# A spatial gating product by seven half-size products per pair of token tiles in place of eight, on one core of Trainium2

## The chip, the cores and the metric

The kernel runs on one core of one Trainium2 chip. A core has five engines with instruction queues of their own: TensorE (PE in the profile; its weight loads are shown apart as PEld), VectorE (DVE), ScalarE (ACT), GpSimd (POOL) and SyncE (SP), which here only issues DMA transfers. Matrix products are written to PSUM, eight banks of 128 partitions by 512 float32 numbers; everything else lies in SBUF. Engines run their own instructions in order and wait for one another by semaphores. The metric is the device time of one launch, in microseconds.

## What is computed

The input x has 2048 tokens of 512 numbers. Two branches are mixed by a gate of each token, `g * a + (1 - g) * b`.

```
# branch a: linear attention, 32 heads of 16
pq, pk = q @ w_phi, k @ w_phi                    # per head
phi = concat([softmax(p), softmax(-p)])          # 32 features
kv, z = sum_s phi_k * v,  sum_s phi_k
a = (phi_q @ kv / (phi_q . z + 1e-6)) @ wo
# branch b: spatial gating, F/2 = 688
z = gelu(x @ w_in); z1, z2 = z[:, :688], layernorm(z[:, 688:])
gate = w_sp @ z2 + b_sp                          # w_sp: 2048 x 2048, over tokens
b = (z1 * gate) @ w_out
```

The change concerns above all `w_sp @ z2`, a product of 2048 x 2048 by 2048 x 688.

## The kernel before

Tokens are handled in 16 tiles of 128. All data is 16-bit (bf16), sums are float32 in PSUM.

The first stage (lines 212 to 334) makes z2 and z1 for four chunks of four tiles. For each z2 tile ScalarE applies gelu, VectorE copies the gate's logit (L204) and takes the mean and variance (L206, L207). `z2_norm` (L262) then has GpSimd compute the reciprocal deviation (L267, `rstd`) and VectorE normalise the four tiles in place (L269). Meanwhile SyncE's queue loads w_sp transposed into `wspT`, 16 slabs of 128 input tokens by 2048 output tokens, in four transfers of 512 output tokens (L154).

The second stage is the loop over 16 key tiles (L580). For each: TensorE multiplies out the next key tile (`k_tile`, L373), ScalarE makes exp(p) and exp(-p) (L356), VectorE sums them per head (L360) and inverts (L376). `even_out` (L366) scales the second half of the features on GpSimd (L369) by the ratio of the two sums (VectorE, L368); the rest of the normalisation is put on v, which VectorE reads out of PSUM (L397). `kv_acc` (L405) adds the tile to the state two tiles later. In each round `gg_next` adds one half-row of the spatial product (`gg_half`, L448): 16 matmuls of 344 columns over all 16 slabs, read out of PSUM by VectorE as (product + bias) * z1 into `ucat` (L456). Six query tiles are also made here (`Q_AT`).

The third stage (L602) makes in each round one query tile, one half-row of the spatial product, one attention tile (L461) and one output tile (`ba_step`, L550). `kvz_evac` (L413) hands the state over between the stages. u, o and eq are transposed by DMA on SyncE's queue. The last 48 of the 688 rows of w_out are handled for four output tiles together (`ba_rem`, L515), next to an attention tile that is split into halves of 64 rows (`attn_tile_64`, L471).

The order of the work on TensorE and ScalarE is the order in which it is written (`manual_schedule`, L576); that on VectorE, GpSimd and SyncE is set by a planner when the program is built. PSUM: in stages two and three six banks rotate under the names mm0 to mm5, two hold the state or an attention tile.

## Time and profile before

| what | value |
| --- | --- |
| three timed executions | 206.29, 206.67, 206.68 us (median 206.67) |
| the profiled execution's span, first to last instruction | 204.3 us; what lies around it up to the median is 2.4 us |
| TensorE busy | 200.5 us in 1557 matmuls |
| VectorE busy | 130.4 us, of it 58.4 from 43.5 to 117 us |
| GpSimd busy | 45.6 us, of it 25.8 from 43.5 to 117 us |
| spatial product's matmuls (L451) | 512, 2.33 us for 16 in the chain of waits |
| granted TensorE clock | 1.000 |

The page names engines and lines; a group `out<-in` gives what is written and read, with partitions x elements and type, the count, the busy time in us, the mean of one in ns, and the engine's idle time just before. A timeline's line begins with start and length in us. Where several instructions are merged (x4), the length is that of them all.

### The profile page before, as it was taken

The numbers are of one execution on the slowest core, as the hardware profiler recorded it, in microseconds if no ns is written. First come the engines' busy times: TensorE is split into PE (matmuls) and PEld (weight loads), VectorE is DVE, ScalarE is ACT, GpSimd is POOL, SyncE is SP. The second block draws the span as 40 slices with busy tenths as digits, with TensorE's granted clock in tenths as the row PEclk, the third lists the DMA queues.
The fourth block names the chain that finished last, engine by engine and source line by source line (L and its number), as shares of the span: only waits on it lengthen the run. The fifth ranks groups of instructions, "written<-read, shape, count | busy, mean of one in ns | idle before, by whom it ended". The sixth has DMA issues, their size and how long they took to land.

```text
span 204.3 us, 3996 instructions
## 1 busy us (share of the span) xinstructions
PE 200.5 (98%) x1557; PEld 119.7 (59%) x1557; DVE 130.4 (64%) x283; ACT 74.6 (37%) x122; POOL 45.6 (22%) x76
## 2 busy tenths in 40 slices
PE   8999999999999999999999999999999999999994
PEld 4666666655665555656565666555555555665642
DVE  4558484838977597979797789555566645633332
ACT  3556677795222333342424042222351136002303
POOL 3020202022523325424242442222204220200000
PEclk9999999999999999999999999999999999999999
DMA  6999399999999027941322229763667458552943
GB/s 200 232 176 153 65 207 232 219 290 231 259 240 232 3 39 158 311 94 21 70 52 41 51 39 115 141 130 59 110 160 80 90 114 183 64 96 51 139 81 104
DMA packets 89947, 27.22 MB, mean 133 GB/s; under 512 B 84200, under 2 KB 89928, under 8 KB 89928
## 3 DMA queue, kind: packets, MB, share of 16 engines
q1 hardware_dynamic: 87616, 24.81, 63.5%
q10 hardware_dynamic: 2312, 2.16, 3.8%
q8 instruction: 12, 0.20, 0.4%
q14 instruction: 7, 0.06, 0.1%
HBM read 4.15 MB, written 2.10 MB: 31 GB/s over the span
## 4 chain that ended last, share of the span: by engine, by line
PE 94%; DMA 4%; SPq 1%; DVE 0%; issue 0%
PE mm L451 37%; PE zp L188 16%; PE mm L352 14%; PE mm L512 9%; PE mm L506 7%; PE mm L392 7%; DMA w_z<-in_B_w_in_dram 2%; PE kvacc L408 2%; PE at L464 2%; DMA xs<-in_A_x_dram 1%; PE mm L517 1%; SPq L131 1%; PE zp L304 0%; SPq L136 0%; PE at L475 0%; PE pq L304 0%
## 5 line engine op out<-in xcount | busy, mean ns | idle before, releaser
L451 PE MATMUL mm<-z2all,wspT 128*128 128x344 bf16 x512 | 79.9, 309 | 0.0
L451 PEld LDWEIGHTS <-wspT 128*128 128x128 bf16 x512 | 49.0, 98 | 25.3
L188 PE MATMUL zp<-w_z,xT 128*128 128x344 bf16 (+1 forms) x254 | 38.1, 309 | 0.1
L356 ACT ACTIVATE eq<-mm 128x512 bf16<-128x512 f32 x32 | 17.4, 595 | 51.4 <-PE mm L352 25.7
L360 DVE TENSOR_REDUCE zs<-eq 128x64 f32<-128x1024 bf16 x16 | 19.5, 1220 | 20.1 <-ACT eq L356 20.1
L188 PEld LDWEIGHTS <-xT 128*128 128x128 bf16 x254 | 24.5, 98 | 12.1 <-issue 0.3
L356 ACT ACTIVATE ek<-mm 128x512 bf16<-128x512 f32 x32 | 17.3, 601 | 27.1 <-PE mm L352 27.1
L456 DVE SCALAR_TENSOR_TENSOR ucat<-mm,bT,z1all 128x344 bf16<-128x344 f32 x32 | 17.4, 544 | 15.1 <-PE mm L451 15.1
L369 POOL TENSOR_TENSOR eq<-eq,ratio 128x512 bf16<-128x512 bf16 x16 | 16.9, 1055 | 44.6 <-DVE ratio L368 36.7
L528 ACT ACTIVATE ob<-mm,g_inv 128x512 bf16<-128x512 f32 (+1 forms) x15 | 10.1, 680 | 33.1 <-PE mm L517 28.5
L360 DVE TENSOR_REDUCE zs<-ek 128x64 f32<-128x1024 bf16 x16 | 19.2, 1208 | 2.8 <-ACT ek L356 2.8
L512 PE MATMUL mm<-wspT,uT 128*128 128x512 bf16 (+2 forms) x85 | 20.1, 367 | 0.0
L352 PEld LDWEIGHTS <-xT 128*128 128x128 bf16 x128 | 12.2, 98 | 12.0
L369 POOL TENSOR_TENSOR ek<-ek,ratio 128x512 bf16<-128x512 bf16 x16 | 16.9, 1055 | 2.2 <-DVE ratio L368 1.7
L506 PE MATMUL mm<-wspT,oT 128*128 128x512 bf16 (+2 forms) x68 | 16.6, 366 | 0.0
L352 PE MATMUL mm<-wq_p,xT 128*128 128x512 bf16 x64 | 16.4, 379 | 0.0
L392 PE MATMUL mm<-wv_sb,xT 128*128 128x512 bf16 x64 | 16.4, 379 | 0.0
L352 PE MATMUL mm<-wk_p,xT 128*128 128x512 bf16 x64 | 16.3, 379 | 0.0
L206 DVE BATCH_NORM_STATS2 bn<-z2all 128x6 f32<-128x344 bf16 x32 | 14.9, 502 | 0.0
L203 ACT ACTIVATE z2all<-zp 128x688 bf16<-128x688 f32 x16 | 11.8, 743 | 7.1 <-PE zp L188 7.0
L257 ACT ACTIVATE z1all<-zp 128x688 bf16<-128x688 f32 x16 | 11.9, 743 | 5.3 <-PE zp L188 4.9
L512 PEld LDWEIGHTS <-uT 128*128 128x128 bf16 x85 | 8.1, 98 | 9.4 <-issue 0.2
(77 smaller groups left out, 142.0 us busy)
## 6 DMA issues: line engine op xcount, KB each, us to landing
out_dram<-ob ACTq DMA_DIRECT2D x12, 128.0 KB, 2.6
wspT<-in_B_w_out_dram SPq DMA_DIRECT2D x2, 640.0 KB, 5.2
w_z<-in_B_w_in_dram SPq DMA_DIRECT2D x2, 344.0 KB, 4.1
wv_sb<-in_A_wqkv_dram SPq DMA_DIRECT2D x1, 512.0 KB
wspT<-in_A_wo_dram SPq DMA_DIRECT2D x2, 256.0 KB, 4.1
out_dram<-ob SPq DMA_DIRECT2D x3, 128.0 KB, 1.8
w_z<-in_B_w_in_dram ACTq DMA_DIRECT2D x2, 172.0 KB, 3.3
w_z<-in_B_w_in_dram SPq DMA_DIRECT2D x2, 172.0 KB, 3.1
```

Source lines behind the costliest of these rows:

```text
L188: nc.tensor.matmul(zp[:, j, 0:n], lhsT=xT[:, dt, tt * P:(tt + 1) * P], rhs=wt[:, dt, j * HF:j * HF + n], start=(dt == 0), stop=(dt == NDT ...
L206: nc.vector.bn_stats(out=bn6[:, tt, j, :], in_=z2v[:, j, :])
L257: nc.scalar.activation(out=z1all[:, tt, :].rearrange("p (j n) -> p j n", j=2), in_=zp[:, :, 0:HF], func=AF.Gelu_apprx_tanh,)
L352: nc.tensor.matmul(ps[:, :], lhsT=xT[:, dt, tt * P:(tt + 1) * P], rhs=w[:, dt, :], start=(dt == 0), stop=(dt == NDT - 1))
L356: nc.scalar.activation(out=e[:, :, a, :], in_=ps[:, :].rearrange("p (h f) -> p h f", f=DH), func=AF.Exp, scale=1.0 - 2.0 * a)
L360: nc.vector.tensor_reduce(out=z[:].rearrange("p h a -> p (h a)"), in_=e[:].rearrange("p h a f -> p (h a) f"), axis=AX.X, op=ALU.add,)
L369: nc.gpsimd.tensor_tensor(out=e[:, :, 1, :], in0=e[:, :, 1, :], in1=ratio[:, :, None].to_broadcast([P, H, DH]), op=ALU.mult)
L392: nc.tensor.matmul(v_ps[:, :], lhsT=xT[:, dt, tt * P:(tt + 1) * P], rhs=wv_sb[:, dt, :], start=(dt == 0), stop=(dt == NDT - 1))
L451: nc.tensor.matmul(gp[:, 0:HF], lhsT=wspT[:, st, tt * P:(tt + 1) * P], rhs=z2all[:, st, j * HF:(j + 1) * HF], start=(st == 0), stop=(st == ...
L456: nc.vector.scalar_tensor_tensor(out=ucat[tt % NU][:, c0 + j * HF:c0 + (j + 1) * HF], in0=gp[:, 0:HF], scalar=bT[:, tt:tt + 1], in1=z1all[ ...
L506: nc.tensor.matmul(acc, lhsT=oTs[tt][:, g, :], rhs=wo_t[:, g, c0:c1], start=start and g == 0, stop=stop and g == NG - 1)
L512: nc.tensor.matmul(acc, lhsT=uTs[tt][:, i + ft, :], rhs=w_main[i][:, ft, c0:c1], start=start and ft == 0, stop=False)
```

## The change

The 16 x 16 blocks of w_sp and the two column halves of z2 are grouped in pairs: two output tiles (rows 1 and 2), even and odd input slabs, two halves of 344 columns. With A11, A12 (row 1, even and odd slabs), A21, A22 (row 2) and B11, B12 (even slabs, column halves), B21, B22 (odd slabs), a pair of output tiles is eight products of eight matmuls over slabs. The change uses Strassen's scheme in Winograd's form with seven: A11 B11, A12 B21, S1 T1, S2 T2, S3 T3, S4 B22, A22 T4, where S1 = A21 + A22, S2 = S1 - A11, S3 = A11 - A21, S4 = A12 - S2, and T1 = B12 - B11, T2 = B22 - T1, T3 = B22 - B12, T4 = B21 - T2. A product's chain is called below by its first factor: chain s2 is S2 T2, chain s4 is S4 B22. In the notation of the code x, y and z are the banks gx, gy and gz.

- `z2_norm` makes the T for its two pairs of slabs with four tensor_tensor operations of 688 elements on VectorE, one of them in place over B12.
- `s_sums` makes the S of a pair of output tiles with four tensor_tensor operations of 1024 elements; S1 takes the place of A21. Those of pair 0 run on VectorE behind the last of `z2_norm`, those of pair 1 on GpSimd behind the last `rstd`, the others on VectorE at the end of the pair two before.
- `products` issues the seven chains of a pair one at a time, in three PSUM banks (gx, gy, gz) that are added into twice or three times, with read-outs between. ScalarE copies the first product; VectorE has six read-outs of 344 columns; GpSimd multiplies 688 and 344 elements by z1. The result u lies in `z1all`, widened to 768 columns, and is transposed into the columns of `wspT` that the pair has used up. Two chains per round replace one half-row, but every fourth round of the key stage has one.
- Keys are normalised by GpSimd over all 1024 features (`k_tile`) with no ratio; v is copied out of PSUM by ScalarE.
- Key, value and query products rotate over three PSUM banks in place of six, four query tiles instead of six are made in the key stage, and the shared remainder and the split attention tile go: each output tile has six full matmuls for u.

```diff
+        zq = z2all[:, ts[0]:ts[-1] + 1, :].rearrange("p (k s) (j n) -> p k s j n", s=2, j=2)
+        tq = tz[:, ts[0] // 2:ts[-1] // 2 + 1]
+        b11, b12, b21, b22 = (zq[:, :, s, j, :] for s in range(2) for j in range(2))
+        for o, a, b in ((tq[:, :, 1, :], b22, b12), (b12, b12, b11),
+                        (tq[:, :, 0, :], b22, b12), (tq[:, :, 2, :], b21, tq[:, :, 0, :])):
+            on_dve = nc.vector.tensor_tensor(out=o, in0=a, in1=b, op=ALU.subtract)
+        return on_dve, on_pool
...
+    def s_sums(p, eng):
+        st = gg.tile([P, 3, 8, P], BF16, name="ssum")
+        a11, a12, a21, a22 = (a_block(p, i, j) for i in range(2) for j in range(2))
+        s2, s3, s4 = (st[:, n] for n in range(3))
+        for o, a, b, op in ((s3, a11, a21, ALU.subtract), (a21, a21, a22, ALU.add),
+                            (s2, a21, a11, ALU.subtract), (s4, a12, s2, ALU.subtract)):
+            eng.tensor_tensor(out=o, in0=a, in1=b, op=op)
+        s_tiles[p] = st
...
+        for p, eng in enumerate((nc.vector, nc.gpsimd)):
+            with tc.issue_after(last[p].ins):
+                s_sums(p, eng)
...
-        return bank_tile(next_turn("mm", 6))
+        return bank_tile(next_turn("mm", 3))
...
-        ek, z = expo(kvp, "ek", 5, tt, wk_p, mm_tile())
-        rk = kvp.tile([P, H, 2], FP32, name="rk", bufs=3)
-        nc.vector.reciprocal(out=rk[:], in_=z[:])
-        even_out(ek, z, rk[:, :, 1])
-        return ek, rk
+        ek, z = expo(kvp, "ek", 4, tt, wk_p, mm_tile())
+        nc.vector.reciprocal(out=z[:], in_=z[:])
+        nc.gpsimd.tensor_tensor(
+            out=ek[:], in0=ek[:], in1=z[:, :, :, None].to_broadcast([P, H, 2, DH]), op=ALU.mult)
+        return ek
...
+        vr = vrs[tt % 3]
+        nc.scalar.copy(out=vr[:, :, 0:64], in_=v_ps[:, :].rearrange("p (u n) -> p u n", n=64))
...
+    def chain(tag, a, b, first, last=True):
+        if first:
+            gt[tag] = bank_tile(tag)[:, 0:HF]
+        for k in range(8):
+            nc.tensor.matmul(gt[tag], lhsT=a[:, k, :], rhs=b[:, k, :], start=first and k == 0,
+                             stop=k == 7, skip_group_check=True)
+        return gt[tag]
+
+    def products(p):
...
+        x = chain("gx", a11, b11, True)
+        nc.scalar.copy(out=p1[:], in_=x)
+        yield
+        y = chain("gy", s2, tt2, True)
+        nc.vector.scalar_tensor_tensor(
+            out=u2[:], in0=y, scalar=bT[:, t1:t1 + 1], in1=p1[:], op0=ALU.add, op1=ALU.add)
+        yield
+        chain("gx", a12, b21, False)
+        nc.vector.scalar_tensor_tensor(
+            out=z1all[:, t1, 0:HF], in0=x, scalar=bT[:, t1:t1 + 1], in1=z1all[:, t1, 0:HF],
+            op0=ALU.add, op1=ALU.mult)
+        yield
+        chain("gy", s3, tt3, False)
+        nc.vector.scalar_tensor_tensor(
+            out=u3[:], in0=y, scalar=bT[:, t2:t2 + 1], in1=p1[:], op0=ALU.add, op1=ALU.add)
+        yield
+        z = chain("gz", s1, tt1, True)
+        nc.vector.tensor_tensor(out=g2[:, 1, :], in0=z, in1=u3[:], op=ALU.add)
+        yield
+        chain("gy", a22, tt4, False)
+        nc.vector.scalar_tensor_tensor(
+            out=g2[:, 0, :], in0=y, scalar=bT[:, t2:t2 + 1], in1=p1[:], op0=ALU.add, op1=ALU.add)
+        nc.gpsimd.tensor_tensor(
+            out=z1all[:, t2, 0:FH], in0=z1all[:, t2, 0:FH], in1=g2[:].rearrange("p j n -> p (j n)"),
+            op=ALU.mult)
+        u_T(t2)
+        yield
+        chain("gz", s4, b22, False)
+        nc.vector.tensor_tensor(out=g1[:], in0=z, in1=u2[:], op=ALU.add)
+        nc.gpsimd.tensor_tensor(
+            out=z1all[:, t1, HF:FH], in0=z1all[:, t1, HF:FH], in1=g1[:], op=ALU.mult)
+        u_T(t1)
+        if p + 2 < NP2:
+            s_sums(p + 2, nc.vector)
+        yield
...
-                ks[tt + 1] = k_tile(tt + 1)
-            ek, rk = ks.pop(tt)
-            pend.append((tt, ek, v_tile(tt, rk)))
+                ks[tt + 1] = k_tile(tt + 1)
+            gg_next(1)
+            pend.append((tt, ks.pop(tt), v_tile(tt)))
             if len(pend) == 3:
                 kv_acc(*pend.pop(0))
-            gg_next(mm_tile())
+            gg_next(0 if tt % 4 == 3 else 1)
...
+            gg_next(1)
+            attn_tile(i + 1)
+            gg_next(1)
```

## The prediction

> **What bounds the kernel now.** I read the page's busy shares and slices first. The third line names the slices of the stage that computes keys and values (44 to 117 us).

> ```profile
> PE 200.5 (98%) x1557; PEld 119.7 (59%) x1557; DVE 130.4 (64%) x283; ACT 74.6 (37%) x122; POOL 45.6 (22%) x76
> ...
> DVE  4558484838977597979797789555566645633332
> ```

> TensorE (PE) is busy from end to end, so work taken off it is gained only if nothing makes it wait. VectorE (DVE) averages 64%, but 7 to 9 tenths in the key and value stage. Next the groups by line and shape, for prices:

> ```profile
> L451 PE MATMUL mm<-z2all,wspT 128*128 128x344 bf16 x512 | 79.9, 309 | 0.0
> ...
> L360 DVE TENSOR_REDUCE zs<-ek 128x64 f32<-128x1024 bf16 x16 | 19.2, 1208 | 2.8 <-ACT ek L356 2.8
> L456 DVE SCALAR_TENSOR_TENSOR ucat<-mm,bT,z1all 128x344 bf16<-128x344 f32 x32 | 17.4, 544 | 15.1 <-PE mm L451 15.1
> ...
> L369 POOL TENSOR_TENSOR ek<-ek,ratio 128x512 bf16<-128x512 bf16 x16 | 16.9, 1055 | 2.2 <-DVE ratio L368 1.7
> ...
> L397 DVE TENSOR_TENSOR vr<-mm,rk 128x512 bf16<-128x512 f32 x16 | 10.9, 684 | 3.2 <-PE mm L392 3.2
> ```

> Zero idle before L451: the 512 matmuls never waited. Then the timeline where GpSimd (POOL) and VectorE touch:

> ```profile
> 113.22 1.06 POOL L369 TENSOR_TENSOR eq<-eq,ratio 128x512 bf16<-128x512 bf16 x1
> 113.46 0.87 DVE L368 TENSOR_TENSOR ratio<-zs,rk 128x32 f32<-128x32 f32 x1
> ```

> The ratio, whose two inputs both lie in SBUF, takes 0.87 us and ends at 114.33, just behind the GpSimd operation (114.28). In the tile's answer its median is 193 ns:

> ```profile
> L368 DVE TENSOR_TENSOR ratio<-zs,rk x16: 139/193/874, 50.0 to 113.5; 128x32 f32<-128x32 f32 x16
> ```

> All six key ratios that start while GpSimd's tensor_tensor runs took 848 to 874 ns; L397 and L456, with one input in PSUM, keep their times there. So VectorE's two-SBUF-input operations and GpSimd's take turns, whole instructions at a time. Last, the timeline where the spatial product begins:

> ```profile
> 41.45 1.04 POOL L267 TENSOR_TENSOR rstd<-veps,mhalf 128x4 f32<-128x4 f32 x1
> 42.52 1.56 DVE L269 TENSOR_SCALAR z2all<-z2all,mv,rstd 128x688 bf16<-128x688 bf16 x4 [1.47 <-POOL rstd L267]
> ...
> 43.49 1.89 PE L352 MATMUL mm<-wk_p,xT 128*128 128x512 bf16 x8
> ...
> 46.08 2.50 PE L451 MATMUL mm<-z2all,wspT 128*128 128x344 bf16 x16
> ```

> **TensorE's work.** A run of 16 L451 matmuls advances 2.33 us in the chain of waits, 0.146 us each; 512 become 448: 64 x 0.146 = -9.3 us. The remainder matmuls shared by four tiles go: in the timeline L517 starts at 145.23 and the next q product at 145.96, 0.73 us for four remainders and a split attention tile (0.82 with the delay in front); instead come four full matmuls (0.216 each: five L512 in 1.08) and eight L464 (0.26), 1.12. Three such groups at +0.3 and +0.2 in the last: +1.1. Net -8.2 us: with no wait anywhere, 206.67 - 8.2 = 198.5.

> **Prices of the new operations.** *GpSimd:* L396 (32 elements, 0.212) and L369 (512, 1.055) give 1.76 ns an element: a sum of s_sums or a whole key tile (1024) 1.95 us, the products with z1 1.36 (688) and 0.76 (344). *VectorE, 16-bit tensor_tensor with both inputs in SBUF:* no row. L269's four take 1.56 (0.37 a step for 688), so 0.55 us for 1024; L397 slopes to 1.22 for 1024. I take 0.61 and 0.44 (688), near L269, which like the new ones is 16-bit and SBUF to SBUF; 1.22 and 0.8 stay as the other end. [...] *PSUM evacuations:* as L456, 0.5 a step.

> **What is nearly free.** ScalarE takes the v copy (0.58, as L311) and p1: per key tile 2 x 0.6 + 0.6 + 0.1 = 1.9 of 4.0 us. VectorE loses L397 and the key ratios (0.68 + 0.44 per tile) and gains per pair six evacuations for four and four sums: about even in time, but the sums are lock-takers. The differences of z2_norm (1.8 us per chunk) in the first three chunks fall into the 1.5 us VectorE idles before the next glog copy: 0 to 0.3 us. On SP the same 16 u transposes now go into dead columns of wspT, each waiting for a GpSimd product (0.8 to 1.4 us); behind them in SP's order stand eqT and oT transposes, which are used two iterations later (some 11 us at 5.6 of TensorE's work each), so this costs nothing until GpSimd is that late; then attention and output tiles wait. The weight loads go one key tile later and lose a 640 KB and a 48 KB piece; they are first read after the last key tile, 30 us on. GpSimd loses the four small kvz copies.

> **The start of the product, +8.1 us.** TensorE comes to the second chain (s2 by T2) at 43.5 + 1.7 (two key tiles) + 1.2 (first chain) + 0.9 (v) = 47.2. VectorE must by then have done four normalisations (1.5), four differences (1.8) and three sums (1.8), from 42.5: 47.6 alone, 0.4 late. But GpSimd issues the four sums of pair 1 at 42.9, right behind rstd and three small memsets (its wspT part has landed: L451 reads it at 46.1). Each operation in both lists waits on its predecessor's semaphore, which opens a gap in which the other engine gets its turn. With turns, GpSimd's four (7.8) lie among VectorE's first eight, and s2 is ready at 42.5 + 5.1 + 7.8 = 55.4: TensorE loses 8.1, some 2.7 at the first chain (last normalisation), the rest at the second. Bounds: 0.4 if GpSimd waits instead; 11.4 at the slow price (four times 0.36 and three times 0.6 more).

> **Each later pair, +2.2 us.** Between chain s4 of a pair and chain s3 of the next, TensorE has three v, two k, three kv, two x and one y runs: 8.6 us. In the built order VectorE does there g1, two reciprocals, four sums, one key reduce and u2: 0.5 + 1.0 + 2.4 + 1.2 + 0.5 = 5.6. GpSimd then has a key tile (1.95), both z1 products (2.1) and soon another key ready; turns put 3 to 4 us between the sums. 9 to 9.5 against 8.6: With each pair's own list (pairs 2 and 3 carry q reduces, but also q products of 0.9 on TensorE) it comes to 0.3, 0.6, 0.8, 0.5 late at pairs 0 to 3. Bounds: 0 without turns, 9 at the slow price (2.4 more in each pair, less in pair 0).

> **The state's hand-over, +3.2 us.** The sums of pair 5 stand ahead of kvz_evac on VectorE. From pair 3's last chain to attention tile 0 TensorE has v, q and three kv (2.5) and two chains (2.3): 4.8. VectorE: g1 0.5, sums 2.4, kvz 0.7, and a q reduce (1.2) ahead of kvz's second half: 4.8; GpSimd's eq and z1 turns add 3.2. Bounds: 0.4 without turns, 5.4 with sums 0.6 longer.

> **Small, +1.2 us:** pair 3's z is read behind two reduces and two reciprocals, 0.7 late; two attention tiles 0.25 each behind sums.

> Sum: -8.2 + 8.1 + 2.2 + 3.2 + 1.2 = +6.5. The durations are of an execution with a span of 204.3; 2.4 us lie around it up to the median 206.67, and I leave them. Forecast **213.2 us**, 3% slower.

> [...]

> **Rivals.**
> 1. *VectorE keeps the port while it has operations in a row, and GpSimd waits.* For it: L269's four run 0.37 us apart without a gap. Against: the new sums wait on each other, and the two directions are seen only from VectorE's side. The start then costs 0.4 plus 2.0 for the first key tile (GpSimd is done with pair 1's sums only at 56), the hand-over 1.1 to 1.4 (one turn each way), the pairs and the small waits 2 to 3.7: -8.2 + 5.4 to 7.5 gives 203.9 to 206. This one ends on the other side; it decides where the start costs under 1.6 us (8.2 less 6.6 elsewhere), that is if not even one GpSimd sum gets in front of s2.
> 2. *All waits are covered,* GpSimd's turns being short: only the 2 us of waits that the order makes without turns: 200.5.
> 3. *The 16-bit tensor_tensor runs at L397's rate.* Start 11.4, the pairs 9, hand-over 5.4, later pairs 3: about 227.

> **How the numbers follow.** The forecast's case holds 0.60 (211 to 218: GpSimd prices 10% either way move it by 2, and a slower restart lies above), rival 1 0.24, rival 2 0.08, rival 3 0.08. The likeliest case alone spans 210 to 218. The range goes down into rival 2 and leaves rival 3 out: 200.5 to 219. Changes under 0.2% (0.4 us) are what a measurement here cannot tell from none. Faster: rivals 1 (nearly all) and 2, with the forecast's lower tail: 0.29; same 0.03; slower 0.68.

> **What would show it.** TensorE idle before the first chain and the s2 chain at 47 to 56 us, released by VectorE; rstd followed by four GpSimd sums that alternate with L278 and L294, some of these lasting 2 us; L436 late. If the VectorE sums keep 0.6 us and GpSimd's stretch, rival 1 holds. The forecast is wrong if GpSimd's sums are much shorter than 1.95, or if VectorE's are over 1.

## The result, and the profile after

The changed kernel takes **216.7 us** (median of four executions, 214.75 to 219.21) against 206.6 in the same session: ratio 1.047, 95% interval 1.042 to 1.052. It is 4.7% slower. The longest of the four, 219.21, counts as a slow execution and is not in the ratio. The forecast was 213.2, its range 200.5 to 219. The profiled execution has a span of 215.1 us, 10.8 more than before.

The busy shares, the granted clock by slices and the chain that ended last, from the page of the changed kernel:

```profile
PE 197.5 (92%) x1469; PEld 115.8 (54%) x1469; DVE 156.9 (73%) x304; ACT 88.4 (41%) x147; POOL 86.7 (40%) x76
...
PEclk9999999997579999999999996999999999999999
...
PE 69%; DVE 21%; DMA 4%; ACT 2%; POOL 2%; issue 1%; SPq 0%; DVEq 0%; POOLq 0%; ACTq 0%
```

TensorE has 88 matmuls fewer but is busy only 3 us less, in a span that is longer: a fifth of the last chain is now VectorE's, and the second line has two dips. In the kernel before it has none:

```profile
PEclk9999999999999999999999999999999999999999
```

What TensorE waits for (line, releaser, us in total, times, longest):

```profile
PE gy L467 <- DVE ssum L294: 7.1, 1, 7.1
PE at L533 <- DVE kvz L441: 2.9, 1, 2.9
PE gx L467 <- DVE z2all L268: 1.0, 1, 1.0
...
PE gy L467 <- DVE u L489: 0.5, 2, 0.3
PE pq L326 <- DVE bT L315: 0.5, 1, 0.5
PE mm L551 <- ACT ob L568: 0.5, 1, 0.5
PE gz L467 <- DVE g L502: 0.4, 1, 0.4
```

One wait of 7.1 us stands out, the second chain of pair 0. The timeline there (start, length, engine, line):

```profile
43.67 7.03 DVE L268 TENSOR_SCALAR z2all<-z2all,mv,rstd 128x688 bf16<-128x688 bf16 x4 [1.47 <-POOL rstd L266]
...
43.78 2.32 POOL L294 TENSOR_TENSOR ssum<-wspT 128x1024 bf16<-128x1024 bf16 x1
...
46.19 2.12 POOL L294 TENSOR_TENSOR wspT<-wspT 128x1024 bf16<-128x1024 bf16 x1
...
48.55 0.31 PE L467 MATMUL gx<-z2all,wspT 128*128 128x344 bf16 x1 [1.00 <-DVE z2all L268]
...
50.58 2.12 POOL L294 TENSOR_TENSOR ssum<-wspT,ssum 128x1024 bf16<-128x1024 bf16 x1
50.73 2.34 DVE L278 TENSOR_TENSOR tz<-z2all 128x688 bf16<-128x688 bf16 x1
53.10 0.52 DVE L278 TENSOR_TENSOR z2all<-z2all 128x688 bf16<-128x688 bf16 x1
...
54.64 0.69 DVE L294 TENSOR_TENSOR ssum<-wspT 128x1024 bf16<-128x1024 bf16 x1
...
56.83 2.48 PE L467 MATMUL gy<-tz,ssum 128*128 128x344 bf16 x8 [7.11 <-DVE ssum L294]
```

Four normalisations that took 1.56 us before take 7.03, and the first difference 2.34 where the others take 0.52. GpSimd's four sums follow one another at 2.2 to 2.4 us; one VectorE instruction gets through between two of them. When GpSimd is done (52.70), VectorE ends the first difference (53.07) and needs 3.7 us more for the other three and three sums; the chain starts at 56.83. It then takes 2.48 us for eight matmuls, 1.33 elsewhere: the clock is halved from 51.43 to 61.67.

The hand-over of the state, with pair 5's sums ahead of `kvz_evac` (L436, L441):

```profile
123.64 1.95 POOL L507 TENSOR_TENSOR z1all<-z1all,g 128x688 bf16<-128x688 bf16 x1
...
124.26 1.87 DVE L294 TENSOR_TENSOR wspT<-wspT 128x1024 bf16<-128x1024 bf16 x1
...
125.55 1.29 POOL L514 TENSOR_TENSOR z1all<-z1all,g 128x344 bf16<-128x344 bf16 x1
...
128.63 1.21 DVE L388 TENSOR_REDUCE zs<-eq 128x64 f32<-128x1024 bf16 x1
...
129.83 0.18 DVE L441 SCALAR_TENSOR_TENSOR kvz<-kvacc,mask 128x32 bf16<-128x32 f32 x1
...
130.16 0.61 PE L533 MATMUL at<-kvz,eqT 128*128 128x68 bf16 x8 [2.92 <-DVE kvz L441]
...
130.58 1.90 PE L380 MATMUL mm<-wq_p,xT 128*128 128x512 bf16 x4
```

VectorE's sums are stretched to 1.87 us and GpSimd's products to 1.95 and 1.29 (1.50 and 0.84 where nothing stands against them). The turns go both ways. Again the matmuls behind the wait run at half the clock: 1.90 us for the four of a query product, 1.03 elsewhere.

### The profile page after: what moved, and what is told of

It is laid out like the page before. It is cut to its first block, busy times and chain, and to the rows that moved or that the text cites. A ratio compares the mean times of both kernels' runs of the same rounds, so it can differ in the third digit from the quotient of the medians.

```text
span 215.1 us, 3862 instructions
## 1 busy us (share of the span) xinstructions
PE 197.5 (92%) x1469; PEld 115.8 (54%) x1469; DVE 156.9 (73%) x304; ACT 88.4 (41%) x147; POOL 86.7 (40%) x76
## 4 chain that ended last, share of the span: by engine, by line
PE 69%; DVE 21%; DMA 4%; ACT 2%; POOL 2%; issue 1%; SPq 0%; DVEq 0%; POOLq 0%; ACTq 0%
PE gy L467 13%; PE mm L380 12%; PE mm L556 9%; PE gz L467 8%; PE gx L467 7%; PE mm L551 6%; PE zp L187 6%; DVE z2all L268 5%; PE mm L421 4%; DVE bn L205 4%; DVE tz L278 3%; DVE ssum L294 3%; DMA w_z<-in_B_w_in_dram 2%; PE at L533 2%; DVE zs L388 2%; POOL rstd L266 1%
## 5 line engine op out<-in xcount | busy, mean ns | idle before, releaser
L397 POOL TENSOR_TENSOR ek<-ek,zs 128x1024 bf16<-128x1024 bf16 x16 | 32.4, 2025 | 25.9 <-DVE zs L396 16.1
L407 POOL TENSOR_TENSOR eq<-eq,ratio 128x512 bf16<-128x512 bf16 x16 | 17.4, 1088 | 46.6 <-DVE ratio L406 29.6
L467 PEld LDWEIGHTS <-wspT 128*128 128x128 bf16 x256 | 24.6, 99 | 15.0 <-issue 1.1
L467 PE MATMUL gy<-tz,ssum 128*128 128x344 bf16 x128 | 22.4, 320 | 7.7 <-DVE ssum L294 7.1
L568 ACT ACTIVATE ob<-mm,g_inv 128x512 bf16<-128x512 f32 (+1 forms) x16 | 10.9, 680 | 44.1 <-PE mm L556 40.8
L467 PEld LDWEIGHTS <-ssum 128*128 128x128 bf16 x192 | 18.4, 99 | 19.0 <-DVE ssum L294 7.6
L388 DVE TENSOR_REDUCE zs<-ek 128x64 f32<-128x1024 bf16 x16 | 19.3, 1208 | 8.1 <-ACT ek L384 6.8
L384 ACT ACTIVATE eq<-mm 128x512 bf16<-128x512 f32 x32 | 17.4, 595 | 18.9 <-PE mm L380 16.0
L467 PE MATMUL gx<-z2all,wspT 128*128 128x344 bf16 x128 | 22.4, 318 | 1.0 <-DVE z2all L268 1.0
L556 PE MATMUL mm<-wspT 128*128 128x512 bf16 (+1 forms) x96 | 22.8, 376 | 0.0
L380 PEld LDWEIGHTS <-xT 128*128 128x128 bf16 x128 | 12.6, 101 | 12.9 <-issue 1.1
L380 PE MATMUL mm<-wq_p,xT 128*128 128x512 bf16 x64 | 17.3, 394 | 0.0
L551 PE MATMUL mm<-wspT,oT 128*128 128x512 bf16 (+1 forms) x64 | 16.2, 376 | 0.7 <-ACT ob L568 0.5
L268 DVE TENSOR_SCALAR z2all<-z2all,mv,rstd 128x688 bf16<-128x688 bf16 x16 | 11.7, 796 | 5.9 <-POOL rstd L266 5.9
L424 ACT CAST vr<-mm 128x512 bf16<-128x512 f32 x16 | 9.4, 586 | 15.9 <-PE mm L421 15.9
L556 PEld LDWEIGHTS <-wspT 128*128 128x128 bf16 x102 | 9.8, 98 | 11.2
```

What stands on the lines that cost most here:

```text
L268: nc.vector.tensor_scalar(out=z2all[:, tt, :], in0=z2all[:, tt, :], scalar1=mv[:, tt, 0:1], scalar2=rstd[:, tt:tt + 1], op0=ALU.subtract, ...
L380: nc.tensor.matmul(ps[:, :], lhsT=xT[:, dt, tt * P:(tt + 1) * P], rhs=w[:, dt, :], start=(dt == 0), stop=(dt == NDT - 1))
L384: nc.scalar.activation(out=e[:, :, a, :], in_=ps[:, :].rearrange("p (h f) -> p h f", f=DH), func=AF.Exp, scale=1.0 - 2.0 * a)
L388: nc.vector.tensor_reduce(out=z[:].rearrange("p h a -> p (h a)"), in_=e[:].rearrange("p h a f -> p (h a) f"), axis=AX.X, op=ALU.add,)
L397: nc.gpsimd.tensor_tensor(out=ek[:], in0=ek[:], in1=z[:, :, :, None].to_broadcast([P, H, 2, DH]), op=ALU.mult)
L407: nc.gpsimd.tensor_tensor(out=eq[:, :, 1, :], in0=eq[:, :, 1, :], in1=ratio[:, :, None].to_broadcast([P, H, DH]), op=ALU.mult)
```

## The experiments

The question was where the saved 8.2 us of TensorE went. *Theory:* into two placements, pair 1's sums on GpSimd just when VectorE has the start to do, and pair 5's sums ahead of the hand-over, together with the lowered clock behind the two pauses. *Rival:* into the sums themselves, which cost their turns wherever they are put.

### Pair 1's sums on VectorE

```diff
-        for p, eng in enumerate((nc.vector, nc.gpsimd)):
-            with tc.issue_after(last[p].ins):
-                s_sums(p, eng)
+        with tc.issue_after(last[0].ins):
+            s_sums(0, nc.vector)
...
+            if tt == 2:      # one sum of pair 1 behind each of four read-outs of pair 0
+                s_sums_behind(1, [(m, 0) for m in ("z1", "u3", "g21", "g20")])
```

> Edit: the four sums of pair 1 are taken off GpSimd and put on VectorE, one each behind four read-outs of pair 0. If turns at the SBUF port make the start late (the theory): VectorE runs its four normalisations, four differences and three sums without a gap, 4 x 0.37 + 4 x 0.54 + 3 x 0.72 = 5.9 us from 43.7, so the second chain starts near 49.7 instead of 56.8, some 1.1 us late instead of 8.4, the clock stays full there (another 2.4), and the four sums cost up to 1 us at later read-outs: 206.5 to 208. If VectorE's own new work were late (rival A): the second chain stays near 56.8 and the time at 216 or above, since VectorE gets four operations more.

Measured: 210.33 us (median of four), ratio 1.022 (1.017 to 1.026). The profiled execution, 213.1, is the longest of the four. Its timeline at the start:

```profile
44.22 1.56 DVE L268 TENSOR_SCALAR z2all<-z2all,mv,rstd 128x688 bf16<-128x688 bf16 x4 [1.48 <-POOL rstd L266]
...
50.10 1.34 PE L477 MATMUL gy<-tz,ssum 128*128 128x344 bf16 x8 [0.99 <-DVE ssum L305]
```

and at the places to which the sums went:

```profile
57.92 2.16 POOL L407 TENSOR_TENSOR ek<-ek,zs 128x1024 bf16<-128x1024 bf16 x1 [0.48 <-DVE zs L406]
...
58.70 1.93 DVE L296 TENSOR_TENSOR wspT<-wspT 128x1024 bf16<-128x1024 bf16 x1
...
62.23 1.33 PE L477 MATMUL gz<-z2all,ssum 128*128 128x344 bf16 x8 [1.21 <-DVE g L512]
...
74.13 1.55 PE L477 MATMUL gy<-tz,ssum 128*128 128x344 bf16 x8 [2.00 <-DVE u L499]
```

The start came out as expected: normalisations unbroken, the second chain 0.99 us late in place of 7.11, no halved clock there. But the time is 2 to 4 us over the expectation. The moved sums wait behind GpSimd's key divisions (1.93 us for one), and a new wait of 1.21 follows. Another, of 2.00, comes behind the sums of pair 2 (one of them takes 2.30); in the changed kernel these cost no more than 0.3, and that the moved sums brought VectorE and GpSimd into this order is likely, not shown. The hand-over's wait of 2.9 us is as before. The profiled execution has two stretches of halved clock, behind these last two waits; by their mean granted clock (0.991 and 0.992 in place of 0.984) the three others, at 210.2 to 210.4, had one. The start is settled as the largest cost. That the sums could be had elsewhere for nothing is refuted.

### Only writes on GpSimd

```diff
+            if eng is nc.gpsimd:
+                for _ in range(2):
+                    eng.memset(o, 0.0)
+            else:
+                eng.tensor_tensor(out=o, in0=a, in1=b, op=op)
```

> Edit: each of GpSimd's four sums of pair 1 is replaced by two memsets of its output, so the sums of pair 1 are left out and GpSimd is busy about as long (eight of some 1 us) but reads nothing in SBUF. Theory (the port that both read through): VectorE's normalisations step by 0.37 us, the second chain starts near 49.7, time some 207. Rival C (a busy GpSimd delays something else, such as the first keys): the second chain is early but TensorE waits 5 us or more at the first state products, time above 212. If memsets take turns too, the normalisations stretch to about 1 us each and the second chain starts near 55.

Measured: 210.0 us (one execution), 3 us above what the theory had and below the rival's 212. Its timeline:

```profile
43.28 2.03 POOL L296 MEMSET wspT<- 128x1024 bf16 x2
43.36 4.43 DVE L268 TENSOR_SCALAR z2all<-z2all,mv,rstd 128x688 bf16<-128x688 bf16 x4 [1.47 <-POOL rstd L266]
...
45.56 5.91 POOL L296 MEMSET ssum<- 128x1024 bf16 x6
...
47.82 0.52 DVE L278 TENSOR_TENSOR tz<-z2all 128x688 bf16<-128x688 bf16 x1
...
49.90 0.69 DVE L298 TENSOR_TENSOR ssum<-wspT 128x1024 bf16<-128x1024 bf16 x1
...
52.10 2.48 PE L471 MATMUL gy<-tz,ssum 128*128 128x344 bf16 x8 [3.85 <-DVE ssum L298]
```

The two kinds of VectorE operation part here. The normalisation (one input in SBUF and one number per partition) takes turns even with an operation that only writes: 4.43 us for four, 1.56 with nothing against them. The differences and sums (two inputs in SBUF) run beside the memsets at 0.52 and 0.69 as if alone. So the expectation failed for the normalisations, which stretched as its last sentence had it, and held for the rest: the second chain starts at 52.10, between its 49.7 and 55. In the changed kernel, where GpSimd's sums read SBUF, both kinds waited (7.03 us for the four normalisations, 2.34 for the first difference). So it is neither GpSimd's instruction count nor its queue, but what each operation does at the memory. Why writes alone hold up the one kind and not the other is not shown, and the port of the expectation stands in no view.

### The same sums on GpSimd, later

```diff
+        scrap1 = pers.tile([P, 1], BF16, name="scrap1")
+        turn1 = nc.gpsimd.tensor_copy(out=scrap1[:, :], in_=s_tiles[0][:, 2, 7, P - 1:P])
+        with tc.issue_after(turn1.ins):
+            s_sums(1, nc.gpsimd)
```

> The changed kernel with one edit: pair 1's four sums stay on GpSimd, all four, but behind a one-column copy that reads the last sum of pair 0, so that they begin when VectorE's work for the start is over. Theory (it is their falling together with VectorE's start work that costs, not that GpSimd makes them): VectorE's normalisations unbroken, the second chain of pair 0 about 1.2 us late, no lowered clock there. The price appears on GpSimd: four sums of 2.12 us end near 59.5 us, the first key tile is divided 2 us later, near 61.5, and the first kv accumulation (due near 59.5 by the trace with pair 1's sums placed on both engines) waits 2 to 3 us; hand-over as in the changed kernel, 3.1 us, and the lowered clock there. Together 7.3 + 2.4 - 1.2 won at the start (the clock in it) and 2 to 3 given back on the changed kernel's 216.7 (span 215.1): 208.5 to 211.5. Rival (GpSimd's sums cost the same wherever they stand, since they delay the keys by as much): 213 or more.

Measured: 214.18 us (four executions), ratio 1.036 (1.033 to 1.039), where the rival had put it. What TensorE waits for:

```profile
PE kvacc L433 <- POOL ek L400: 3.1, 1, 3.1
PE at L536 <- DVE kvz L444: 2.9, 1, 2.9
PE gy L470 <- DVE u L501: 2.0, 1, 2.0
PE gy L470 <- DVE ssum L294: 1.0, 1, 1.0
```

The start is cured here too (1.0), so the falling together did cost what it seemed to. But four sums are 8.7 us of GpSimd, and the keys stand behind them: the first accumulation waits 3.1. The second step was missed in the expectation: VectorE, held in its queue at a key reduction for 7.3 us until the first division was over, reads pair 0 out late (2.0), and a stretch of halved clock (60.99 to 67.81) begins in the first wait and holds the second. Just behind the start GpSimd had no room for all four.

### The hand-over alone

```diff
-        if p + 2 < NP2:
+        if p + 2 < NP2 and p != 3:
...
-        kvz_evac()
+        with tc.issue_after(kvz_evac().ins):
+            s_sums(5, nc.vector)
```

> Edit: the four sums of pair 5 are issued behind the state's hand-over on VectorE instead of ahead of it. If those sums and GpSimd's turns between them delay the hand-over (the theory): TensorE's 3.1 us wait at attention tile 0 falls to under 0.6 and the second drop of the clock (1.25 us) goes with it: 212.3 to 213. If the state itself is late (rival B: GpSimd's normalising of the last key tiles, or a q reduce): the wait stays at 2 us or more and the time above 215.5.

Measured: 214.49 us, ratio 1.038 (1.035 to 1.041): 0.9% off the changed kernel's ratio of 1.047, but 1.5 us above the theory's range. The wait of 2.9 us at the first attention tile is gone and so is the second stretch of halved clock, but the sums now hold up the attention's read-out:

```profile
131.29 0.41 PE L533 MATMUL at<-kvz,eqT 128*128 128x68 bf16 x8 [1.58 <-DVE o L538]
```

Half of the wait moved on by one tile. With the sums spread, as in the version with both placements moved below, 0.2 of it is left.

### The clock alone

36 matmuls whose result nobody reads fill the pause before the second chain; nothing gets earlier.

```diff
+        if p == 0:
+            idle = bank_tile("gy")[:, 0:HF]
+            for k in range(36):
+                nc.tensor.matmul(idle, lhsT=a11[:, k % 8, :], rhs=b11[:, k % 8, :], start=True, stop=True,
+                                 skip_group_check=True)
```

> Edit: 36 matmuls of 344 columns whose result is overwritten are put in front of the second chain, 5.3 us of work inside TensorE's 7.3 us pause. They do not move the second chain (56.8). If the pause costs more than itself because the granted clock halves from 51.4 to 61.7 us (theory): the clock stays at 1.00 there, the second chain and what follows run at 0.146 and 0.216 us a matmul: 2.4 us less, 214.3. If the halved clock costs nothing that ends late (rival D): 216.7.

Measured: 214.86 us, ratio 1.040 (1.038 to 1.043), 1.8 us less by medians and 2.2 by the spans (212.9). The second chain started 0.2 us earlier (56.66), as the first stage had ended that much earlier, and ran in 1.34 us in place of 2.48. From its start to the wait at the hand-over TensorE needs 68.2 us, in the changed kernel 70.4. The halved clock at the start costs about 2 us by itself.

### Keys and values alone, in the kernel before

```diff
-        even_out(ek, z, rk[:, :, 1])
...
+        nc.gpsimd.tensor_tensor(
+            out=ek[:], in0=ek[:], in1=z[:, :, :, None].to_broadcast([P, H, 2, DH]), op=ALU.mult)
...
+        nc.scalar.copy(out=vr[:, :, 0:64], in_=v_ps[:, :].rearrange("p (u n) -> p u n", n=64))
```

> The kernel before with one part of the change alone: keys divided by both sums on GpSimd (1024 elements in place of 512), v copied from PSUM by ScalarE with its ones columns set once, no ratio for the keys. Eight half products of 16 matmuls as before. Theory (GpSimd and ScalarE have room in the stage of keys, and TensorE waits for neither): GpSimd's key operations 2.0 us each, no new wait of TensorE over 0.3 us, 206.2 to 206.9 us, the same as before (206.5) within 0.2%. Rival (the keys arrive too late for the accumulation, or the longer GpSimd operations hold up VectorE's ratio for the queries): kv accumulation waits for the last keys at the hand-over by 1 us or more, 207.5 us or more.

Measured: 206.31 us in twelve executions, ratio 0.9995 (0.9983 to 1.0008): no difference. GpSimd's division takes 1.93 us each, VectorE is busy 115.8 us in place of 130.4, and TensorE waits for nothing. This part of the change costs nothing by itself, and takes 15 us off VectorE.

### Both placements moved

Pair 1's first two sums stay on GpSimd behind the gate of the run above, the other two go to VectorE, one behind each of two read-outs; `kvz_evac` gets ahead, and pair 5's sums are issued two behind each of the first two attention read-outs (`s_part(p, n, eng)` issues the n-th sum of pair p).

```diff
+        with tc.issue_after(turn1.ins):
+            s_part(1, 0, nc.gpsimd)
+            s_part(1, 1, nc.gpsimd)
...
+                with tc.issue_after(read[('u2', 0)].ins):
+                    s_part(1, 2, nc.vector)
+                with tc.issue_after(read[('g21', 0)].ins):
+                    s_part(1, 3, nc.vector)
...
+        with tc.high_priority():
+            kvz_evac()
...
+                with tc.issue_after(read[('o', 0)].ins):
+                    s_part(5, 0, nc.vector)
+                    s_part(5, 1, nc.vector)
```

> Three moves together, nothing else altered: of pair 1's four sums the first two stay on GpSimd but are queued behind a one-column copy that reads the last sum of pair 0, so that they begin only when VectorE's work for the start is over; the other two go to VectorE, one behind the u2 and one behind the g2 of pair 0; kvz_evac goes ahead of everything that VectorE has at the hand-over, and pair 5's four sums go behind the first two attention tiles. Theory (the change lost its gain to the two placements, the start and the hand-over, and not to the sums as such): the four normalisations before pair 0's sums in one unbroken 1.6 us, the second chain about 1.2 us late, no pause long enough to lower the granted clock, the waits before later pairs 1 to 2.5 us together, the hand-over under 0.8 us. With the full TensorE floor of 198.5 us and the 1.0 us of the tail that is 203 to 206 us, at or under the kernel before (206.5). Rival (turns at the memory cost the same wherever the sums are put, so that what is taken from the start appears later, as 3.5 us did when pair 1's sums went to VectorE as a whole): waits of 8 to 9 us in all and 208 to 210 us.

Measured: **204.08 us** (203.62 to 204.60, five executions) beside 206.35 of the kernel before: ratio 0.988 (0.986 to 0.990). Not one piece of arithmetic differs from the changed kernel. From its page, the granted clock by slices:

```profile
PEclk9999999999999999999999999999999999999999
```

and all waits of TensorE behind the first 2 us:

```profile
PE gy L479 <- DVE u L510: 1.4, 1, 1.4
PE gy L479 <- DVE ssum L296: 1.0, 1, 1.0
...
PE mm L563 <- DMA oT<-o: 0.7, 2, 0.4
PE pq L334 <- DVE bT L323: 0.5, 1, 0.5
PE gz L479 <- DVE g L514: 0.4, 1, 0.4
PE gy L479 <- DVE u L501: 0.3, 1, 0.3
PE at L545 <- DVE o L550: 0.2, 1, 0.2
```

VectorE has two operations more than in the changed kernel, GpSimd two sums less. The waits shown are 4.5 us, where the changed kernel's lines above have 12.9, no pause lowers the clock, and the attention tiles wait 0.2 in place of 2.9. The theory holds; the rival (208 to 210) falls.

### The bias copy

```diff
-        nc.vector.tensor_copy(out=bT[:, :], in_=bt[:, :])
+        nc.scalar.copy(out=bT[:, :], in_=bt[:, :])
```

> The version with both placements moved, and the one copy of the bias row (PSUM to SBUF, 16 columns) given from VectorE to ScalarE. VectorE's queue holds it behind three of the new differences of the second chunk, and the folded projection's first matmul waits 0.54 us for it. Theory (that wait is the change's cost in the first stage): the fold starts unhindered and the time falls by 0.4 to 0.7 us from 204.1, to 203.4 to 203.7. Rival (the wait is taken up by the next one, since VectorE or ScalarE is as late as before at the end of the stage): 204.0 to 204.2.

Measured: 204.46 us, ratio 0.989 (0.988 to 0.991), not to be told from the run above; the theory's 203.4 to 203.7 is refuted. The copy is early, but the wait reappears under another name:

```profile
27.88 0.15 DVE L203 COPY glog<-zp 128x1 f32<-128x1 f32 x1
...
28.09 1.18 PE L187 MATMUL zp<-w_z,xT 128*128 128x344 bf16 x7 [0.52 <-DVE glog L203]
```

What is late is VectorE, by the four differences of 0.52 us; whichever copy out of PSUM comes next behind them is waited for.

## Why the prediction was right, and which terms were off

The direction, the place and the size of the largest wait were right; the total was 3.5 us low. The prediction's terms beside the trace (from one matmul's start to the next beyond the usual 0.146 or 0.216 us, which is about 0.15 more than the idle time in the views):

| step | predicted | measured |
| --- | --- | --- |
| TensorE's work | -8.2 | -8.2 (below) |
| start of the product | +8.1 | +8.4 |
| later pairs | +2.2 | +0.9 |
| hand-over | +3.2 | +3.1 |
| pair 3's z; attention tiles | +0.7; +0.5 | +0.6; none seen |
| halved clock behind two pauses | left out of the sum | +3.9 |
| tail, last two outputs | nothing | +1.0 |
| fold behind the first-stage differences | 0 to 0.3 | +0.5 |
| first weight load | nothing | +0.6 |
| sum | +6.5 | +10.8 (spans: +10.8) |

The times differ by 10.1 us only. In all later executions on record 1.7 to 1.8 us lie around the span, not the 2.4 that the prediction took; so the profiled execution before was probably some 0.7 us shorter than the median one.

**TensorE's work.** It can be read best where the clock never falls. The version with both placements moved has a span of 202.9; before it was 204.3. Less 8.2, plus its waits of 4.5 and 0.15 for each of eight restarts, that is 201.8. Its first stage is 1.5 us longer (the last normalisations start at 44.01, before at 42.52), of which the wait there and its restart are 0.7; where the other 0.8 comes from is not shown. With it: 202.6. The number of matmuls was the right price, to some 0.4 us.

**Start.** The mechanism is shown: turns at the memory, whole instructions long, between GpSimd's sums and VectorE's operations. Its split was off. The prediction put 2.7 us at the first chain, for the last normalisation; that chain uses even slabs only and waited for the third, 1.2 us. All four GpSimd sums passed before VectorE's second difference, at 2.12 each where 1.95 was taken; the differences and sums behind them took 0.52 and 0.69 where 0.44 and 0.61 was taken. GpSimd got its turns also without a gap in VectorE's list: the normalisations, 0.37 us apart before, took turns too (7.03 us for four). That the errors cancelled is luck. Rivals 1 and 3 fall by the same lines: GpSimd gave way for 0.2 us at its first sum (2.32 in place of 2.12) and no more, and 0.69 is far from 1.22.

**Later pairs, the mis-sized term: 0.9 in place of 2.2.** The prediction let turns put 3 to 4 us between the four sums of a pair. VectorE's sums in the changed kernel, by what they read (last columns: busy us, mean ns, idle before):

```profile
L294 DVE TENSOR_TENSOR ssum<-wspT 128x1024 bf16<-128x1024 bf16 x14 | 13.1, 939 | 0.1
...
L294 DVE TENSOR_TENSOR wspT<-wspT 128x1024 bf16<-128x1024 bf16 x7 | 10.2, 1460 | 0.2
...
L294 DVE TENSOR_TENSOR ssum<-wspT,ssum 128x1024 bf16<-128x1024 bf16 x7 | 4.8, 690 | 0.1
```

Four sums take 2 x 0.94 + 1.46 + 0.69 = 4.0 us against 2.8 undisturbed: 1.3 us of turns in the mean pair. Pair 0's, which had nothing against them, are in that mean; those of pairs 2 to 5, which stand where the term has its turns, were stretched by 1.9, 2.0, 1.3 and 2.4 us. For a turn GpSimd must have an operation ready, and between the first and the last sum of pairs 2 and 3 it was busy for half of the time. That this is why the turns were fewer is argued; no run tests it. The term's own sum was loose too: 5.6 and 3 to 4 are 8.6 to 9.6, where it has 9 to 9.5.

**Hand-over.** As predicted in mechanism (sums, then a query reduction, ahead of kvz's second half). The size is partly luck: four sums of 5.1 us in all, where the prediction had 2.4 and 3.2 of turns, and some 0.4 us of small operations and gaps that it did not have. The two runs that moved it show that the order on VectorE is the cause.

**The clock, the term that was left out.** The prediction's sum has no term for it: the trace before has a granted clock of 1.000 and no pause from which to price one. Only the range of its likeliest case, up to 218, has room for "a slower restart"; no row of that trace shows one, and the runs showed 2.4 and 1.5 us in its place. From 56.83 to 61.67 every matmul took double its step, 2.4 us lost; behind the hand-over 1.5 more (129.93 to 133.35). The run with matmuls in the pause shows the first of these by itself (1.8 to 2.2), and one of the four executions of the changed kernel, 214.75 us at a mean granted clock of 0.984 in place of 0.968, had about half of the halved time and was 1.9 us shorter than the next. The halved stretches last 3.41, 6.83 or 10.24 us (129.93 to 133.35 in the changed kernel, 60.99 to 67.81 with the sums later on GpSimd, 51.43 to 61.67 in the changed kernel). The pause of 7 us brought the longest of them, of which 4.8 us had matmuls in them. With the 3.9 us the forecast would have been 217.1. That the rest comes out within 0.4 us is luck in part: 1.9 too much at later pairs, z and attention tiles stands against 2.1 for the tail, the fold and the weight load.

**Small.** The tail was costed at nothing, because transposes in SyncE's order are used two iterations later. At the end no work is left to cover: 1.0 us, 0.7 of idle time also in the version with both placements moved. The differences of the second chunk do not all fit into VectorE's idle time before the fold, as the prediction had them at 0 to 0.3: three of them stand ahead of the bias copy and one behind it. The late weight load is not the change's; it is missing in other executions with the same first stage.

## What to carry to other kernels

Before moving element-wise work to an idle GpSimd, look at what VectorE does at that moment: what counted here was not how busy either engine is, but whether their SBUF operations meet just ahead of a matmul (four normalisations took 7.03 us in place of 1.56). Moving ten instructions, most of them within their own queue, turned a change of +4.7% into one of -1.2%, but each single move gave back part of its gain at the next full queue (the keys, the read-outs, the attention tiles); spread the work over several gaps and look at all waits again after each move. A pause of TensorE can cost more than its length: add half of the time for which matmuls then run at the lowered clock (2.4 of 4.8 us here).

## What the runs showed that was not expected

Pauses shorter than the shortest halved stretch (3.41 us) lowered the clock: 2.9 us at the hand-over of the changed kernel (halved from 129.93 to 133.35) and 2.0 us in the run with pair 1's sums on VectorE (halved from 75.10 to 78.52). But the length alone does not decide. In the run with memsets the hand-over's pause was as long, and the clock, lowered once near the start, stayed full there (121.56 to 124.50; the clock by slices and the wait):

```profile
PEclk9999999999799999999999999999999999999999
...
PE at L537 <- DVE kvz L445: 2.9, 1, 2.9
```

Two smaller things:

- GpSimd's memset of 1024 elements holds up VectorE's normalisation (4.43 us for four in place of 1.56) and not VectorE's two-input operations (0.52 and 0.69 us, as elsewhere).
- Moving a copy of 16 columns from VectorE to ScalarE removed a wait of 0.54 us and brought one of 0.52 at the next copy in line.
